# A scan with a gated linear unit on one core: a new written-out order of engines and transfers, with five gated buffers and separate gate loads

## The chip, the cores and the metric

The kernel runs on one core of one Trainium2 chip. Its time is device microseconds of one launch; the median of several runs is compared. A profile is one further execution, recorded by the hardware profiler, whose own time stands beside its span below.

## What is computed

Four sequences of 6336 tokens with 256 channels pass through a gated linear recurrence and then through a gated unit with a causal convolution of five taps.

```python
a_base  = sigmoid(a_param)
a_t     = exp(8 * sigmoid(r_gate) * log(clip(a_base, 1e-6, 1 - 1e-6)))
norm    = sqrt(max(1 - a_t * a_t, 1e-6))
x_gated = norm * sigmoid(i_gate) * x
h = a_t[:, t] * h + x_gated[:, t];  y[:, t] = h      # for each t, in float32
gate = sigmoid(causal_conv5(y, moe_conv_w))
out  = (gate * (y @ moe_w_val)) @ moe_w_out
```

x, r_gate, i_gate and the output are (4, 6336, 256) float32, 26 MB each. The weights are two 256 x 256 matrices, five rows of taps and one decay parameter per channel.

## The kernel before

The 25,344 tokens are cut into 27 chunks: one of 512, 23 of 1024, two of 512 and one of 256. A chunk passes through a pipeline over all engines. Steps up to the scan are by chunk c and channel half h; steps after it are by chunk and by part s of 512 tokens.

- `ldri`, `ldx` (L216 to L224): SyncE starts the loads of r and i, as a pair, into six gate slots (three chunks deep), and of x into two x slots.
- `tanh` (L290): ACT turns both gates into tanh(g/2), in bf16, in one instruction.
- `srT` (L295): TensorE transposes the r part to channel rows; `exp` (L304): ACT makes a from it, into a ring of five.
- `e` (L310): POOL squares a, into a ring of five; `sq` (L354): ACT makes the root of 1 - a*a, scaled by 1/4 inside. It is done for up to three chunks at a time, because it needs another function table than tanh and exp: a table load stands ahead of it and another behind it (L472).
- `s1` (L318): POOL adds 1 to the i part; `u` (L345): POOL multiplies it with x, into a ring of four gated buffers. For chunks 0 and 1 this is done another way: TensorE passes x through an identity in float32 (`xc`, L327) and VectorE does the sum and product from there (`ux`, L335).
- `nT` (L367), `xg` (L374), `xgT` (L382): TensorE transposes the root to token rows, VectorE multiplies the gated buffer with it in place, and TensorE transposes that back to channel rows.
- `scan` (L395): VectorE runs the recurrence along the tokens.
- `conv` (L407), `tg` (L417): TensorE does the five taps as matmuls with diagonal weights; ACT takes tanh into a ring of two.
- `val` (L425), `gv` (L430): TensorE multiplies with the first weight; VectorE forms the gated product into a second ring of two.
- `out` (L439), `osbD` (L454) or `osbA` (L450): TensorE multiplies with the second weight; VectorE or ACT copies the result to SBUF, into a ring of five.
- `store` (L459): ACT's queue starts the transfer to memory.

Ahead of the loop the decay constant is made from `a_param` by one exp, three small VectorE steps and one ln (L252 to L263). The weights are loaded once (`ldw`) and cast to bf16 by three ACT instructions (`wc`, L282 and L284).

The order is written out in the string `PLAN`, as names with chunk, part and PSUM bank. The program walks through it and emits one step after another under a manual schedule, so each engine, and each queue that starts transfers, works through its own steps in the order of the string. Waits between engines follow from the buffers: a load of r waits until `srT` has read the slot's former chunk, a load of i until `u` has, a load of x until `u` has read the x slot; a `u` waits until `xgT` has read the gated buffer's former chunk. Transfers of both queues (SyncE for loads, ACT for stores) share eight completion semaphores in turn, so one can also wait until an earlier transfer that has the same semaphore has landed.

The rings are set by numbers at the top.

```python
NRI = 3      # chunks of gate slots
NX = 2       # x
NA = 5       # a
NE = 5       # squares and roots
NU = 4       # gated buffers
NTG = 2      # tanh of the convolution
NGV = 2      # gated product
```

Of the kernel before, what the change touches and what calls it, by code (L numbers as in the profile page):

```python
# [8 lines left out]
P = 128  # L9
HP = 64  # L10
# [6 lines left out]
X_PE = [0, 1]  # L17
NRI = 3
NX = 2
NA = 5  # L20
NE = 5
NU = 4
NY = 3
NOSB = 5
NTG = 2
NGV = 2
# [7 lines left out]
ldri.0.-1 ldri.1.-1 ldx.0.-1 ldx.1.-1 ldri.2.-1 ldw.-1 tanh.0.-1 srT.0.0.7 srT.0.1.5 exp.0.1.-1 exp.0.0.-1 e.0.0.-1  # L34
tanh.1.-1 e.0.1.-1 xc.0.1.0 xc.0.0.6 ux.0.0.-1 xc.1.2.1 u.0.-1 sq.0.1.-1 ux.1.2.-1 srT.1.0.0 ldri.3.-1 xc.1.1.5
ldx.2.-1 nT.0.0.7 srT.1.1.4 exp.1.0.-1 xg.0.0.-1 ux.1.1.-1 exp.1.1.-1 xc.1.0.0 tanh.2.-1 xc.1.3.5 e.1.1.-1 ux.1.0.-1
e.1.0.-1 wc.-1 srT.2.0.3 s1.2.-1 srT.2.1.2 xgT.0.0.4 exp.2.0.-1 scan.0.0.-1 exp.2.1.-1 e.2.0.-1 u.1.-1 tanh.3.-1
ldx.3.-1 ldri.4.-1 e.2.1.-1 u.2.-1 srT.3.1.3 srT.3.0.6 xgT.0.1.1 sq.1.2.-1 s1.3.-1 ldx.4.-1 ldri.5.-1 nT.2.0.7
nT.2.1.0 u.3.-1 xg.2.0.-1 exp.3.1.-1 xg.2.1.-1 nT.1.1.7 scan.0.1.-1 nT.1.0.5 tanh.4.-1 xg.1.1.-1 conv.0.0.0 xg.1.0.-1
xgT.2.0.3 e.3.1.-1 ldx.5.-1 xgT.1.1.4 ldri.6.-1 xgT.1.0.2 scan.1.1.-1 tg.0.0.-1 exp.3.0.-1 s1.4.-1 srT.4.1.1  # L40
exp.4.1.-1 scan.1.0.-1 val.0.0.4 e.3.0.-1 tanh.5.-1 srT.4.0.6 gv.0.0.-1 conv.1.0.0 u.4.-1 scan.2.0.-1 xgT.2.1.7
tg.1.0.-1 srT.5.1.5 srT.5.0.4 exp.4.0.-1 scan.2.1.-1 val.1.0.0 exp.5.1.-1 e.4.1.-1 ldx.6.-1 ldri.7.-1 exp.5.0.-1
gv.1.0.-1 conv.2.0.6 tanh.6.-1 e.5.1.-1 out.0.0.4 conv.1.1.0 osbD.0.0.-1 e.4.0.-1 val.2.0.2 tg.1.1.-1 val.1.1.4
e.5.0.-1 store.0.0.-1 tg.2.0.-1 out.1.0.0 conv.2.1.6 osbD.1.0.-1 s1.5.-1 sq.3.3.-1 gv.1.1.-1 u.5.-1 gv.2.0.-1
out.2.0.0 out.1.1.4 osbD.2.0.-1 osbD.1.1.-1 s1.6.-1 nT.3.1.3 ldri.8.-1 nT.3.0.2 ldx.7.-1 val.2.1.0 tg.2.1.-1 xg.3.0.-1
xg.3.1.-1 store.1.0.-1 u.6.-1 tanh.7.-1 gv.2.1.-1 xgT.3.1.7 nT.4.0.6 scan.3.1.-1 srT.6.0.1 srT.6.1.4 xgT.3.0.2
nT.4.1.0 nT.5.1.5 exp.6.0.-1 xg.4.0.-1 s1.7.-1 ldri.9.-1 xg.4.1.-1 exp.6.1.-1 srT.7.0.1 xg.5.1.-1 ldx.8.-1 nT.5.0.6
scan.3.0.-1 exp.7.0.-1 out.2.1.4 e.6.1.-1 tanh.8.-1 xgT.4.1.3 srT.7.1.7 xg.5.0.-1 conv.3.0.0 e.7.0.-1 osbD.2.1.-1
scan.4.1.-1 conv.3.1.4 u.7.-1 store.1.1.-1 tg.3.0.-1 xgT.4.0.6 srT.8.0.2 tg.3.1.-1 scan.4.0.-1 srT.8.1.0 exp.7.1.-1
val.3.1.4 exp.8.1.-1 gv.3.1.-1 e.6.0.-1 conv.4.1.6 ldx.9.-1 exp.8.0.-1 ldri.10.-1 xgT.5.0.3 store.2.0.-1 tg.4.1.-1  # L50
out.3.1.4 e.7.1.-1 scan.5.0.-1 tanh.9.-1 xgT.5.1.7 val.3.0.0 e.8.0.-1 conv.4.0.2 gv.3.0.-1 osbD.3.1.-1 e.8.1.-1
tg.4.0.-1 scan.5.1.-1 val.4.1.4 s1.8.-1 val.4.0.0 sq.6.3.-1 out.3.0.2 gv.4.1.-1 u.8.-1 gv.4.0.-1 osbD.3.0.-1 out.4.0.0
out.4.1.2 osbD.4.0.-1 srT.9.1.6 osbD.4.1.-1 nT.8.1.5 s1.9.-1 ldri.11.-1 nT.6.1.4 xg.8.1.-1 exp.9.1.-1 conv.5.0.2
ldx.10.-1 xg.6.1.-1 store.3.0.-1 tanh.10.-1 e.9.1.-1 nT.6.0.4 nT.7.1.1 xg.6.0.-1 nT.7.0.0 xgT.6.1.5 xg.7.0.-1 u.9.-1
xgT.6.0.4 xg.7.1.-1 srT.9.0.6 scan.6.0.-1 nT.8.0.7 exp.9.0.-1 conv.5.1.0 tg.5.0.-1 scan.6.1.-1 tg.5.1.-1 xgT.7.1.2
s1.10.-1 ldri.12.-1 store.2.1.-1 tanh.11.-1 val.5.1.0 ldx.11.-1 xg.8.0.-1 srT.10.1.3 srT.10.0.6 gv.5.1.-1 e.9.0.-1
val.5.0.4 conv.6.1.0 gv.5.0.-1 exp.10.1.-1 u.10.-1 srT.11.1.7 scan.7.1.-1 store.3.1.-1 store.4.1.-1 conv.6.0.4
tg.6.1.-1 exp.10.0.-1 srT.11.0.1 xgT.7.0.0 tg.6.0.-1 val.6.0.2 scan.7.0.-1 exp.11.0.-1 e.10.0.-1 out.5.0.4 ldri.13.-1
store.4.0.-1 ldx.12.-1 exp.11.1.-1 osbD.5.0.-1 out.5.1.0 e.10.1.-1 tanh.12.-1 conv.7.0.6 osbD.5.1.-1 e.11.0.-1
val.6.1.4 gv.6.0.-1 gv.6.1.-1 out.6.0.2 tg.7.0.-1 e.11.1.-1 store.5.1.-1 osbD.6.0.-1 xgT.8.1.6 xgT.8.0.7 s1.11.-1  # L60
out.6.1.4 scan.8.1.-1 sq.9.3.-1 val.7.0.2 u.11.-1 gv.7.0.-1 osbD.6.1.-1 conv.7.1.2 scan.8.0.-1 srT.12.0.1 srT.12.1.6
nT.9.0.0 nT.9.1.4 s1.12.-1 ldri.14.-1 nT.11.0.5 xg.9.0.-1 exp.12.0.-1 nT.10.0.7 ldx.13.-1 xg.9.1.-1 store.6.1.-1
xg.11.0.-1 store.5.0.-1 tg.7.1.-1 xgT.9.1.0 e.12.0.-1 scan.9.1.-1 exp.12.1.-1 out.7.0.2 tanh.13.-1 val.7.1.4 u.12.-1
osbD.7.0.-1 conv.8.0.0 gv.7.1.-1 nT.10.1.2 xgT.9.0.3 xg.10.1.-1 tg.8.0.-1 srT.13.0.6 scan.9.0.-1 s1.13.-1 ldri.15.-1
store.7.0.-1 tanh.14.-1 val.8.0.0 ldx.14.-1 out.7.1.4 xg.10.0.-1 e.12.1.-1 conv.8.1.2 gv.8.0.-1 srT.13.1.7 osbD.7.1.-1
store.6.0.-1 tg.8.1.-1 u.13.-1 xgT.10.0.1 srT.14.0.0 scan.10.0.-1 exp.13.0.-1 srT.14.1.4 out.8.0.2 exp.14.0.-1
xgT.10.1.6 store.7.1.-1 osbD.8.0.-1 exp.13.1.-1 conv.9.0.0 e.14.0.-1 exp.14.1.-1 scan.10.1.-1 ldx.15.-1 val.8.1.2
ldri.16.-1 tg.9.0.-1 nT.11.1.7 val.9.0.4 e.13.0.-1 store.8.0.-1 tanh.15.-1 gv.8.1.-1 conv.9.1.0 gv.9.0.-1 e.14.1.-1
out.8.1.2 val.9.1.4 osbD.8.1.-1 tg.9.1.-1 e.13.1.-1 xg.11.1.-1 store.8.1.-1 gv.9.1.-1 xgT.11.0.3 out.9.0.0 s1.14.-1
sq.12.3.-1 scan.11.0.-1 out.9.1.6 xgT.11.1.5 u.14.-1 osbD.9.1.-1 osbD.9.0.-1 val.10.0.6 srT.15.1.4 scan.11.1.-1  # L70
conv.10.0.2 s1.15.-1 nT.12.1.1 ldri.17.-1 tg.10.0.-1 nT.12.0.0 xg.12.1.-1 ldx.16.-1 srT.15.0.5 exp.15.1.-1 xg.12.0.-1
conv.10.1.2 gv.10.0.-1 u.15.-1 exp.15.0.-1 xgT.12.0.0 val.10.1.6 scan.12.0.-1 tg.10.1.-1 nT.13.1.1 store.9.0.-1
tanh.16.-1 conv.11.0.4 gv.10.1.-1 nT.13.0.3 e.15.0.-1 ldri.18.-1 nT.14.0.0 xg.13.1.-1 out.10.1.6 ldx.17.-1 xg.14.0.-1
xg.13.0.-1 tg.11.0.-1 e.15.1.-1 srT.16.0.2 osbD.10.1.-1 out.10.0.0 tanh.17.-1 val.11.0.6 osbD.10.0.-1 s1.16.-1
xgT.12.1.3 gv.11.0.-1 srT.16.1.1 conv.11.1.4 u.16.-1 scan.12.1.-1 exp.16.1.-1 val.11.1.6 tg.11.1.-1 srT.17.1.0
exp.16.0.-1 gv.11.1.-1 xgT.13.0.5 srT.17.0.4 store.10.0.-1 exp.17.1.-1 conv.12.0.2 scan.13.0.-1 e.16.0.-1 ldri.19.-1
store.9.1.-1 exp.17.0.-1 nT.14.1.0 ldx.18.-1 xgT.13.1.7 tg.12.0.-1 xg.14.1.-1 e.17.1.-1 scan.13.1.-1 store.10.1.-1
tanh.18.-1 out.11.0.2 xgT.14.0.4 e.16.1.-1 conv.12.1.0 osbD.11.0.-1 val.12.1.6 scan.14.0.-1 e.17.0.-1 tg.12.1.-1
out.11.1.2 val.12.0.0 s1.17.-1 gv.12.1.-1 sq.15.3.-1 gv.12.0.-1 out.12.1.6 u.17.-1 osbD.11.1.-1 out.12.0.4
# [61 lines left out]
def kernel(  # L141
# [54 lines left out]
    with tc.manual_schedule():  # L196
# [16 lines left out]
        def slot(c, e):  # L213
            return 2 * (c % NRI) + e

        def op_ldri(k, bank):  # L216
            c = k[0]
            n = CHUNKS[c]
            for e, src in ((0, rf), (1, if_)):
# [287 lines left out]
```

## Time and profile before

| what | us |
|---|---|
| median of 3 runs | 310.08 (309.9 to 310.13) |
| the profiled execution's own time | 311.12 |
| its span in the profile | 309.0 |
| VectorE, scans (L395), 54 | 115.8 busy |
| ScalarE, gate tanh (L290), 27 | 90.2 busy |
| POOL, gated product u (L345), 25 | 96.0 busy |
| POOL, squares (L310), 54 | 93.6 busy |
| TensorE, conv matmuls (L407), 1224 | 65.3 busy |
| transfers, 104.74 MB | 339 GB/s over the span |

Busy time of an engine is the time in which at least one of its instructions ran; an instruction that overlaps its neighbour is counted once. A group of instructions shares a line, an engine and an operation. "Idle before" is the time an engine sat idle just ahead of an instruction, and the releaser is what the trace shows to have ended it. A store or a load is started by a queue (ACTq, SPq), which isn't counted as busy, and lands microseconds later.

### The profile page before, as it was taken

The page shows a single profiled execution, that of the slowest core. Times are in us where ns is not written, and L with a number is a line of the kernel's source. Part 1 is how long each engine was busy: PE and PEld are TensorE (multiplying, and loading weights), DVE is VectorE, ACT ScalarE, POOL GpSimd, SP SyncE. Part 2 cuts the span into 40 slices and gives each one's busy share as a digit, 9 for nine tenths or more (in the row PEclk, how much of TensorE's full clock was granted, in tenths as well). Part 3 has the DMA queues.
Part 4 walks back from the last instruction along what each step waited for, and adds up shares of the span by engine and source line. Part 5 has one row for each costly group of instructions (what it writes and reads, how often), then busy time and mean ns, then how long its engine had stood idle before and what let it go on. Part 6 is the DMA issues. An engine that isn't in the chain of part 4 may idle for free.

```text
span 309.0 us, 6335 instructions
## 1 busy us (share of the span) xinstructions
PE 248.1 (80%) x2627; PEld 167.7 (54%) x2627; DVE 252.3 (82%) x208; ACT 278.5 (90%) x185; POOL 235.2 (76%) x118
## 2 busy tenths in 40 slices
PE   0582577958888898799489998988899987999994
PEld 0232454447546564557257665675666655565763
DVE  1052079479898989999499999999999998989893
ACT  6799999999999999998699999999999979868632
POOL 3229998997998999899996799989959993038000
PEclk9995589999999999999979999999999999999999
DMA  7999999998997999999999997999897764182555
GB/s 288 427 360 422 382 417 364 365 352 318 389 377 263 413 414 422 421 421 421 428 423 365 363 390 280 376 426 424 336 369 309 285 249 137 69 337 109 200 212 237
DMA packets 19466, 104.74 MB, mean 339 GB/s; under 512 B 2151, under 2 KB 2670, under 8 KB 10606
## 3 DMA queue, kind: packets, MB, share of 16 engines
q1 hardware_dynamic: 12224, 78.39, 65.0%
q10 hardware_dynamic: 7214, 25.96, 21.0%
q8 instruction: 20, 0.33, 0.4%
q14 instruction: 8, 0.07, 0.1%
HBM read 78.39 MB, written 25.95 MB: 338 GB/s over the span
## 4 chain that ended last, share of the span: by engine, by line
PE 24%; DMA 21%; POOL 18%; ACT 17%; issue 11%; DVE 6%; ACTq 1%; SPq 1%; POOLq 0%; DVEq 0%
DMA gate<-in_i_gate_dram 13%; POOL uring L345 10%; PE pp L407 7%; PE pp L439 6%; DMA xr<-in_x_dram 6%; ACT gate L290 5%; POOL ering L310 5%; ACT tgr L417 4%; PE pp L425 4%; ACT aring L304 4%; POOL gate L318 3%; PE pp L367 3%; DMA out_dram<-osb 3%; DVE yring L395 3%; PE pp L327 2%
## 5 line engine op out<-in xcount | busy, mean ns | idle before, releaser
L310 POOL TENSOR_TENSOR ering<-aring 128x1024 f32<-128x1024 f32 (+2 forms) x54 | 93.6, 1754 | 36.7 <-ACT aring L304 35.1
L395 DVE TENSOR_TENSOR_SCAN yring<-aring,yring,pp 128x1024 bf16<-128x1024 f32 (+2 forms) x52 | 113.4, 2193 | 4.1 <-PE pp L382 4.1
L345 POOL TENSOR_TENSOR uring<-gate,xr 128x2048 bf16<-128x2048 bf16 (+2 forms) x25 | 96.0, 3845 | 4.3 <-PE pp L382 2.6
L290 ACT ACTIVATE gate<-gate 128x4096 bf16<-128x4096 f32 (+2 forms) x27 | 90.2, 3340 | 7.6 <-DMA xr<-in_x_dram 3.9
L407 PE MATMUL pp<-yring,diag 64*64 64x512 bf16 (+13 forms) x1224 | 65.3, 341 | 5.2 <-DVE yring L395 2.2
L430 DVE SCALAR_TENSOR_TENSOR gvr<-tgr,pp 128x1024 bf16<-128x1024 bf16 (+1 forms) x50 | 59.4, 1200 | 8.9 <-ACT tgr L417 6.7
L439 PE MATMUL pp<-wo,gvr 128*128 128x256 bf16 x396 | 52.7, 279 | 13.9 <-DVE gvr L430 7.9
L304 ACT ACTIVATE aring<-pp,khf 128x1024 f32<-128x1024 bf16 (+2 forms) x54 | 59.3, 1144 | 3.9 <-PE pp L295 2.2
L417 ACT ACTIVATE tgr<-pp 128x1024 bf16<-128x1024 f32 (+1 forms) x50 | 50.5, 1024 | 10.0 <-PE pp L407 8.6
L439 PEld LDWEIGHTS <-gvr 128*128 128x128 bf16 x396 | 42.5, 115 | 23.8 <-DVE gvr L430 11.1
L425 PE MATMUL pp<-yring,wv 128*128 128x512 bf16 (+1 forms) x200 | 50.5, 377 | 6.1 <-DVE osb L454 2.2
L454 DVE COPY osb<-pp 128x1024 f32<-128x1024 f32 x41 | 49.0, 1211 | 6.1 <-PE pp L439 5.9
L318 POOL TENSOR_SCALAR gate<-gate 128x2048 bf16<-128x2048 bf16 (+2 forms) x25 | 44.5, 1781 | 5.4 <-ACT gate L290 5.4
L407 PEld LDWEIGHTS <-diag 64*64 64x64 bf16 x1224 | 30.6, 107 | 30.6 <-issue 14.5
L354 ACT ACTIVATE ering<-ering,b 128x4096 bf16<-128x4096 f32 (+4 forms) x16 | 46.4, 2932 | 0.1
L374 DVE TENSOR_TENSOR uring<-uring,pp 128x1024 bf16<-128x1024 bf16 (+1 forms) x50 | 32.0, 672 | 12.7 <-PE pp L367 12.5
L295 PE MATMUL pp<-ident_b,gate 128*128 128x128 bf16 x396 | 31.4, 229 | 13.2 <-ACT gate L290 11.1
L295 PEld LDWEIGHTS <-gate 128*128 128x128 bf16 x396 | 26.6, 103 | 21.9 <-ACT gate L290 14.0
L367 PE MATMUL pp<-ident_f,ering 128*128 128x128 f32 x198 | 32.3, 303 | 5.4 <-ACT ering L354 3.9
L382 PE MATMUL pp<-ident_f,uring 128*128 128x128 f32 x198 | 31.5, 282 | 6.1 <-ACT tgr L417 2.8
L367 PEld LDWEIGHTS pp<-ident_f,ering 128*128 128x128 f32 x198 | 27.8, 208 | 11.6 <-ACT ering L354 4.8
L425 PEld LDWEIGHTS <-wv 128*128 128x128 bf16 x200 | 18.8, 98 | 23.9 <-issue 11.1
(33 smaller groups left out, 86.9 us busy)
## 6 DMA issues: line engine op xcount, KB each, us to landing
out_dram<-osb ACTq DMA_DIRECT2D x49, 512.0 KB, 7.9
gate<-in_r_gate_dram SPq DMA_DIRECT2D x23, 1024.0 KB, 11.7
gate<-in_i_gate_dram SPq DMA_DIRECT2D x23, 1024.0 KB, 9.6
xr<-in_x_dram SPq DMA_DIRECT2D x23, 1024.0 KB, 10.0
gate<-in_r_gate_dram SPq DMA_DIRECT2D x3, 512.0 KB, 7.7
gate<-in_i_gate_dram SPq DMA_DIRECT2D x3, 512.0 KB, 10.7
xr<-in_x_dram SPq DMA_DIRECT2D x3, 512.0 KB, 3.4
yring<-in_moe_w_val_dram SPq DMA_DIRECT2D x1, 256.0 KB
```

The source lines that it names most:

```text
L290: nc.scalar.activation(out=tgate[:, s0:s0 + 2, 0:w], in_=gate[:, s0:s0 + 2, 0:w], func=ACT.Tanh, scale=0.5)
L295: nc.tensor.transpose(out=ppb[:, bank * 2 * BANK + j * P:bank * 2 * BANK + (j + 1) * P], in_=tgate[:, slot(c, 0), j * D + h * P:j * D + (h ...
L304: nc.scalar.activation(out=dst, in_=src, func=ACT.Exp, scale=khf[:, h:h + 1], bias=khf[:, h:h + 1])
L310: nc.gpsimd.tensor_tensor(out=ering[:, c % NE, h * n:(h + 1) * n], in0=a, in1=a, op=ALU.mult)
L345: nc.gpsimd.tensor_tensor(out=u, in0=t, in1=xt, op=ALU.mult)
L367: nc.tensor.transpose(out=pp[:, d0:d0 + P], in_=src[:, w, :], identity=ident_f[:])
L395: nc.vector.tensor_tensor_scan(out=yring[:, h, y0:y0 + n], data0=aring[:, c % NA, h, 0:n], data1=src, initial=prev, op0=ALU.mult, op1=ALU.add)
L407: nc.tensor.matmul(out=pp[col * HP:(col + 1) * HP, b0 + d0:b0 + d1], lhsT=diag[r * HP:(r + 1) * HP, h, kk, :], rhs=yring[r * HP:(r + 1) * ...
L417: nc.scalar.activation(out=tgr[:, nth[k] % NTG, :, 0:n], in_=two(live["conv", k], n), func=ACT.Tanh, scale=0.5)
L425: nc.tensor.matmul(out=pp[:, (bank + m) * BANK:(bank + m) * BANK + n], lhsT=wv[:, hk, m, :], rhs=yring[:, hk, y0:y0 + n], start=(hk == 0), ...
L430: nc.vector.scalar_tensor_tensor(out=gvr[:, nth[k] % NGV, :, 0:n], in0=tgr[:, nth[k] % NTG, :, 0:n], scalar=1.0, in1=two(live["val", k], n ...
L439: nc.tensor.matmul(out=pp[:, bank * BANK + j * D:bank * BANK + (j + 1) * D], lhsT=gvr[:, nth[k] % NGV, m, 0:n].rearrange("c (p q) -> c q p ...
```

## The change

The order string is another one throughout, and with it come some changes of code. In words:

- `ldri` is split into `ldr` and `ldi`, which stand in the string by themselves. Loads start with r of chunk 0, i of 1, i of 0, r of 1. Later, loads of r stand one or two chunks ahead of loads of i (r of 7, 8 and 9, then i of 7 and x of 6, then i of 8).
- A common function `dma` starts all transfers, and adds an edge from each transfer to the one before it in the string, across both queues. The edge is of a kind that makes no semaphore wait; it holds the order in which the transfers are taken.
- POOL leaves the set of engines of the manual schedule; its instructions are wrapped in `keep`, which holds them in the order of the program.
- `X_PE` is empty: chunks 0 and 1 get `s1` and `u` on POOL like the others, and `xc` and `ux` go.
- `NU` is 5 for 4. `gvr` goes: `gv` writes in place of `tg`'s result, whose ring is 3 for 2.
- `tanh` of chunk 0 is two instructions (`tanh` for r, `tanhi` for i).
- The weight casts `wc` go from ACT to POOL.
- The decay constant is made by exp, ln(1 + v) and two VectorE steps after it, with the limits of the clip moved behind the logarithm. Three small VectorE steps ahead of it go. Some constants are put into the last output buffer until it is first used.
- Of the 50 output copies ACT makes 14 for 9 (parts 17.0, 18.0, 22.0, 22.1 and 24.0 and 23.1 are added, 20.1 is taken away), VectorE 36 for 41.
- Stores stand in groups at places: 0.0, 1.0, 1.1 and 2.0 follow each other on ACT's queue after `tanh` of chunk 7 and ahead of one `exp` and `tanh` of chunk 8; 8.1, then one `exp`, then 9.0, 9.1 and 10.0 stand ahead of `tg` of 11.0 and `tanh` of chunk 16.
- On POOL, `u` of chunks 4, 7, 10 and 13 stands behind the four squares of the two chunks after it in the root's batch, which it preceded, in whole or in part, before.

The root's batches are the same (chunk 0; 1 and 2; then threes; 21 and 22; 23 and 24; 25 and 26), and the number of table loads too (24). The diff, cut to its core:

```diff
-X_PE = [0, 1]
+X_PE = []
-NU = 4
+NU = 5
-NTG = 2
-NGV = 2
+NTG = 3
...
-    with tc.manual_schedule():
+    with tc.manual_schedule(engines={mybir.EngineType.SP, mybir.EngineType.Activation, mybir.EngineType.DVE,
+                                     mybir.EngineType.PE}):
...
-        def op_ldri(k, bank):
+        keep = tc.keep_in_program_order
+        turn = []
+
+        def dma(queue, dst, src):
+            i = queue.dma_start(dst, src)
+            if turn:
+                tc.add_manual_dep(i.ins, turn[-1].ins.name,
+                                  mybir.DependencyInfo(mybir.DependencyClass.NoSync, mybir.DependencyReason.DATA),
+                                  reason="turn of the transfers")
+            turn.append(i)
+
+        def op_ldr(k, bank):
             c = k[0]
             n = CHUNKS[c]
-            for e, src in ((0, rf), (1, if_)):
-                nc.sync.dma_start(gate[:, slot(c, e), 0:n * H].rearrange("p (j d) -> p j d", d=D), toks(src, c, 0, n))
+            dma(nc.sync, gate[:, slot(c, 0), 0:n * H].rearrange("p (j d) -> p j d", d=D), toks(rf, c, 0, n))
+
+        def op_ldi(k, bank):
+            c = k[0]
+            n = CHUNKS[c]
+            dma(nc.sync, gate[:, slot(c, 1), 0:n * H].rearrange("p (j d) -> p j d", d=D), toks(if_, c, 0, n))
...
-        nc.vector.tensor_scalar(out=ksig[:], in0=kex[:], scalar1=1.0, scalar2=None, op0=ALU.add)
-        nc.vector.reciprocal(out=ksig[:], in_=ksig[:])
-        nc.vector.tensor_scalar(out=ksig[:], in0=ksig[:], scalar1=1e-6, scalar2=1.0 - 1e-6,
-                                op0=ALU.max, op1=ALU.min)
-        nc.scalar.activation(out=kln[:], in_=ksig[:], func=ACT.Ln)
+        nc.scalar.activation(out=kln[:], in_=kex[:], func=ACT.Ln, bias=1.0)
...
         def op_wc(k, bank):
             for hk in range(H):
-                nc.scalar.copy(out=wv[:, hk, :, :].rearrange("p m (i c) -> p i m c", i=2),
-                               in_=wvf[:, hk, :].rearrange("p (i m c) -> p i m c", i=2, m=2))
-            nc.scalar.activation(out=wo2[:], in_=wof, func=ACT.Copy, scale=0.5)
+                keep(nc.gpsimd.tensor_scalar(out=wv[:, hk, :, :].rearrange("p m (i c) -> p i m c", i=2),
+                                             in0=wvf[:, hk, :].rearrange("p (i m c) -> p i m c", i=2, m=2),
+                                             scalar1=1.0, scalar2=1.0, op0=ALU.mult, op1=ALU.mult))
+            keep(nc.gpsimd.tensor_scalar(out=wo2[:], in0=wof, scalar1=0.5, scalar2=1.0, op0=ALU.mult, op1=ALU.mult))
...
-            s0 = slot(c, 0)
-            nc.scalar.activation(out=tgate[:, s0:s0 + 2, 0:w], in_=gate[:, s0:s0 + 2, 0:w], func=ACT.Tanh, scale=0.5)
+            s0, s1 = slot(c, 0), slot(c, 0) + (1 if c == 0 else 2)
+            nc.scalar.activation(out=tgate[:, s0:s1, 0:w], in_=gate[:, s0:s1, 0:w], func=ACT.Tanh, scale=0.5)
+
+        def op_tanhi(k, bank):
+            c = k[0]
+            w = CHUNKS[c] * H
+            nc.scalar.activation(out=tgate[:, slot(c, 1), 0:w], in_=gate[:, slot(c, 1), 0:w], func=ACT.Tanh, scale=0.5)
...
-            nc.gpsimd.tensor_tensor(out=u, in0=t, in1=xt, op=ALU.mult)
+            keep(nc.gpsimd.tensor_tensor(out=u, in0=t, in1=xt, op=ALU.mult))
...
-            nc.vector.scalar_tensor_tensor(out=gvr[:, nth[k] % NGV, :, 0:n], in0=tgr[:, nth[k] % NTG, :, 0:n], scalar=1.0,
+            nc.vector.scalar_tensor_tensor(out=tgr[:, nth[k] % NTG, :, 0:n], in0=tgr[:, nth[k] % NTG, :, 0:n], scalar=1.0,
                                            in1=two(live["val", k], n), op0=ALU.add, op1=ALU.mult)
...
-            nc.scalar.dma_start(toks(of, c, o, n),
-                                osb[:, nth[k] % NOSB, 0:n // P * D].rearrange("p (q d) -> p q d", d=D))
+            dma(nc.scalar, toks(of, c, o, n), osb[:, nth[k] % NOSB, 0:n // P * D].rearrange("p (q d) -> p q d", d=D))
```

## The prediction, made before the changed kernel was run

> **What bounds the kernel now.** I read the page first: busy shares, then the span in forty slices.
>
> ```profile
> PE 248.1 (80%) x2627; PEld 167.7 (54%) x2627; DVE 252.3 (82%) x208; ACT 278.5 (90%) x185; POOL 235.2 (76%) x118
> ...
> PE   0582577958888898799489998988899987999994
> DVE  1052079479898989999499999999999998989893
> ACT  6799999999999999998699999999999979868632
> POOL 3229998997998999899996799989959993038000
> ```
>
> ACT has the most work, and its idle 30.5 us (309.0 - 278.5) lies at the two ends and in one dip near slice 19. No engine is at rest in the middle. So I asked for the busy time by stage.
>
> ```profile
> 0.00:60.00 60.00, 35.83 (x272) 22.25 (x273) 23.31 (x27) 53.81 (x37) 41.73 (x27) 0.86 0.96 379
> 60.00:100.00 40.00, 30.92 (x333) 22.27 (x333) 35.96 (x30) 39.90 (x23) 37.05 (x18) 1.00 0.92 341
> 100.00:160.00 60.00, 48.62 (x523) 32.92 (x522) 53.97 (x41) 55.55 (x33) 58.13 (x27) 0.97 1.02 420
> 160.00:250.00 90.00, 81.95 (x921) 57.01 (x919) 88.95 (x70) 89.66 (x57) 80.41 (x37) 1.00 0.92 356
> 250.00:309.00 59.00, 50.72 (x584) 33.24 (x584) 50.14 (x43) 39.53 (x39) 17.85 (x13) 0.99 0.49 190
> ```
>
> The columns are the stretch, its length, then the busy us of PE, weight load, DVE, ACT and POOL, the granted clock, the share of the transfers and GB/s. Four regimes follow. To 60 us the pipeline fills and the DMA is nearly full (0.96). From 100 to 160 the DMA is full (420 GB/s) and ACT loses 4.45 us. From 160 to 250 ACT (89.66 of 90) and DVE (88.95) are full together. From 250 on ACT has 19.5 us idle, while DVE (50.14) and PE (50.72 of 59) carry the backlog; finer stretches show PE at 10.00 of 10.00 from 280 to 290 and from 290 to 300. The timeline of ACT shows the loss near 146:
>
> ```profile
> 144.80 1.07 ACT L417 ACTIVATE tgr<-pp 128x1024 bf16<-128x1024 f32 x1
> 149.31 0.34 ACTq L459 DMA_DIRECT2D out_dram<-osb  x1
> 149.78 3.62 ACT L290 ACTIVATE gate<-gate 128x4096 bf16<-128x4096 f32 x1 [3.90 <-DMA xr<-in_x_dram]
> ```
>
> The gate tanh of chunk 15 doesn't read x. A store stands ahead of it on ACT's queue, and its issue came at 149.31, just before the tanh starts. In the compiled order that store waits for the transfer some eight earlier to land. The tanh itself needs i of chunk 15, issued only at 136.0, when POOL's gate product of chunk 12 had freed the slot. Late release, a full DMA, and waits on an engine's queue: that is one loss of 3.90 us.
>
> **What the Trainium skill says.** "DMA: Bandwidth & Descriptors", section Anatomy of one DMA: the wait of a transfer is done by the sequencer that issues it, before dispatch; the trace agrees, with SyncE's queue waiting 88.7 us for POOL at L220 and the tanh above behind a store. Same page, Where 436 GB/s comes from: a ceiling of 435 GB/s; the best 20 us stretch here, 140 to 160, moved 424. "Advanced Engine Details and Errata", section Engine Queue Depths: eight instructions for ScalarE; the trace fits, since a store was issued at 62.97 while a sqrt from 61.21 was still running, so a short wait at a store need not idle ACT.
>
> **The change part by part.** The sum is made against the profiled execution: span 309.0 in a time of 311.12, 1.04 above the median 310.08. I carry differences in us over to the median unchanged.
>
> *Head, -1.9.* The weight casts leave ACT: 0.69 + 0.63 = 1.3 us (L282, L284), on ACT's own path from the first tanh on. The six x matmul groups (L327, 12 instructions, 8.8 us of PE) and six DVE products (L335, 4.2 us) go. They lie where DVE sat idle 10.69 us, so DVE gains nothing; PE's release takes with it the 0.60 us that ACT waited for a transpose behind them. The other head waits of ACT (0.54, 1.13, 0.48, 1.03) I leave: r, i of chunk 1 still need the same 3.0 MB ahead, chunk 2 the same 6.5 MB. The split tanh of chunk 0 and the three DVE steps gone from the decay constant (0.17 each) end before that load lands: nothing. Bounds: 0 and -(1.3 + 3.8) = -5.1.
>
> *POOL, 0.* It receives s1 and u of chunks 0 and 1 (1.05 + 2.16 + 1.90 + 4.12 = 9.2 us) and the weight casts, 1024 elements a partition. L318 has 1.90 us for 2048 bf16 elements, so 0.95; at the two-input fp32 price of the "GPSIMD Engine Reference", section Performance versus the Vector engine (4497 ns for 2048), 2.25. I take 1.0. POOL is idle 3.76 us before 10.3 and 8.85 us before 21.2, which covers the 9.2; without that cover u of chunk 2, and the loads behind it, come 9.2 later. The casts stand after those gaps, ahead of u of chunk 3, the step that frees i and x slots: 0 to +2.25 there, taken as 0: u of chunk 3 ended at 40.9, a load of i takes 9.6, and the tanh of chunk 6 started only at 54.4.
>
> *Loads, -2.0.* r and i no longer go as a pair. r of chunks 8 and 9 is put ahead of i of chunk 7, and so on: r needs only PE's transposes done, i needs POOL's u. The fifth gated buffer lets u run one chunk further ahead of the transposes back (POOL waited 2.6 us for these). The number of loads, 84 on SyncE, and the bytes stay. To 160 us the DMA was busy 0.96 x 60 + 0.92 x 40 + 1.02 x 60 = 155.6 us, so at most 4.4 us of earlier arrival is there; the head has taken 1.9 of it. Of ACT's stalls of 3.90 and 0.45 I take 2.0 back; bounds 0 and -4.35. Against it: in POOL's new order u of every third chunk (4, 7, 10, 13) stands behind four squares, 4 x 1.87 = 7.5 us later, and i of the third chunk after waits for it.
>
> *Copies, +1.0.* ACT makes 14 output copies for 9. Two of them (17.0, 18.0) lie in the stage where ACT is full: 2 x 1.01 = 2.0. DVE, just as full, loses 2 x 1.21. Bounds 0 and +2.0; I take the middle.
>
> *DVE and the backlog, -3.0.* Net five copies of 1.211 leave DVE, 6.05 us. What is late next is PE: it was idle 90 - 81.95 = 8.05 us from 160 to 250 and 2.12 + 1.35 + 0.38 = 3.85 from 250 to 300, mostly waiting for DVE and ACT. DVE's relief can turn at most 6.05 of these 11.9 into work; I take half. Bounds 0 and -6.05.
>
> *Stores and turns, 0.* The edges between transfers add no waits of their own (the compiled order shows none across the queues), but they fix which earlier transfer each one waits for. Stores now stand up to four in a row on ACT: 0.0, 1.0, 1.1 and 2.0 after the tanh of chunk 7, with an exp and the tanh of chunk 8 behind them and all POOL work on chunk 8 behind these; 9.0, 9.1 and 10.0 likewise ahead of the tanh of chunk 16. Each is worth 0 (transfer eight earlier landed) to 3.9 us (the stall above). Less than nothing it can't be here, since that gain is counted under the loads. I take 0, since the copies for most of them end well before.
>
> *One ring for tg and gv, 0.* tg now waits for the output matmuls three steps back instead of a DVE product two back: between -1.3 (ACT's present wait for L430) and +1.0 (one group of L439).
>
> Table loads stay at 24 in both orders. Sum: -1.9 - 2.0 + 1.0 - 3.0 = -5.9: 305.2 for the profiled execution, **304.2** for the median.
>
> **The rivals.**
> - *PE keeps the end where it is*: the DVE relief meets a PE that is full at 10.00 of 10.00 from 280 on, and gives nothing: 310.1 - 1.9 - 2.0 + 1.0 = 307.2. For it: PE has no copy taken away. Against: 8 us of its idle lie before 250.
> - *Everything comes through*: both stalls and all of DVE's relief, copies free: 310.1 - 1.9 - 4.35 - 6.05 = 297.8. Against: ACT alone has 278.5 - 1.3 + 5.0 = 282 us of work, and this leaves it only some 15 us idle.
> - *Slower: stores hold ACT.* One mechanism: a store on ACT's queue waits for a transfer eight back, the tanh behind it waits too, and POOL and the next loads with it. Price 3.9 us a time. It decides from 5.9 / 3.9 = 1.5, so from two new stalls: 304.2 + 7.8 = 312.0. For it: four stores in a row. Against: the queue holds several instructions, and only one of 50 stores cost ACT such a stall before.
> - *No effect*: DMA-bound to 160, PE-bound after, only the places of waits change: 310.1.
>
> **How the numbers follow.** Forecast 304.2 with 0.52, PE at the end 0.20, everything 0.13, stores 0.11, no effect 0.04. A change of 0.2% (0.6 us) is about what a measurement can tell from none. Faster is the first three, 0.85; same 0.04; slower 0.11. The range leaves out the stores and the no-effect case (0.15) and reaches from just below the best case to just under no change: 297.5 to 309.4.
>
> **What would show it.** Right: ACT idle from 100 to 160 falls from 4.45 to about 2.5; the third square root batch starts near 59, not 61.2 (1.9 earlier); DVE busy about 241; PE idle from 160 on falls by some 3. Wrong: POOL idle before a u at a wait for x, ACT gaps just behind L221 stores, or a tail after the last gate tanh longer than now.

## The result and the profile after

| | us, median | runs |
|---|---|---|
| before | 310.11 | 309.9 to 311.11 |
| after | 319.31 | 317.74 to 319.62 |

The ratio is 1.028 (95% interval 1.0239 to 1.0321): slower by 9.2 us, where 304.2 was predicted. The profiled execution of after took 319.1 us, with a span of 317.3: 8.3 us longer than the span before. First, the same lines of the page as before:

```profile
PE 244.4 (77%) x2585; PEld 170.9 (54%) x2615; DVE 243.4 (77%) x195; ACT 283.2 (89%) x188; POOL 245.6 (77%) x125
...
PE   1153385785898888899849967999779999998994
DVE  0030179379987999899668988699998999989972
ACT  6798999999999999997977978999898899889754
POOL 3898997989998799899867989994999854743000
```

The work moved as the diff says. VectorE has 8.9 us less, POOL 10.4 more, ScalarE 4.7 more. But the 9s of ACT's row break up from slice 20 on, where the row before was solid. The stages show the same in microseconds; the columns are again stretch, length, busy us of PE, weight load, DVE, ACT and POOL, clock, share of the transfers and GB/s.

```profile
0.00:60.00 60.00, 28.45 (x258) 21.20 (x261) 18.14 (x19) 53.21 (x35) 50.06 (x33) 1.00 0.90 368
60.00:100.00 40.00, 30.93 (x317) 22.15 (x316) 34.20 (x28) 38.43 (x22) 38.40 (x18) 0.96 0.93 360
100.00:160.00 60.00, 52.26 (x588) 36.19 (x588) 55.06 (x44) 57.63 (x35) 54.78 (x25) 1.00 0.94 371
160.00:250.00 90.00, 73.18 (x759) 51.53 (x772) 79.53 (x63) 80.59 (x49) 77.32 (x36) 0.94 0.94 369
250.00:317.30 67.30, 59.62 (x687) 39.85 (x684) 56.42 (x46) 53.34 (x50) 25.06 (x16) 0.98 0.50 190
```

From 100 to 160 us ScalarE's idle time fell from 4.45 to 2.37 us, as predicted. From 160 to 250 it rose from 0.34 to 9.41 us; VectorE's busy time fell by 9.4 there and TensorE's by 8.8. This stage loses what the whole change costs.

A second way to count needs no borders of stages. ScalarE runs the square roots in eleven batches, the same in both kernels, and from the start of the last batch to its last instruction it takes 22.4 us before and 22.1 after. So the end follows from that start, which is ScalarE's busy time ahead of it plus its idle time ahead of it. Before: 266.2 + 17.4 = 283.6. After: 268.1 + 24.2 = 292.3. The change adds 1.9 us of work and 6.8 us of idle time ahead of the last roots. The largest piece lies between the sixth batch of roots and the seventh: 6.9 us for 0.1. The other pieces nearly cancel. The stretch from the sixth batch to the seventh, first before, then after:

```profile
155.60:186.40 30.80, 28.50 (x315) 19.43 (x313) 30.20 (x23) 30.73 (x20) 26.43 (x12) 0.97 1.00 384
156.10:202.10 46.00, 34.52 (x369) 23.76 (x371) 36.47 (x28) 39.06 (x24) 38.55 (x16) 0.93 0.97 387
```

(The new order also puts 8.3 us more of ScalarE's work into this stretch; later stretches have less.)

What was waited for? The waits of SyncE's queue, which starts all loads; first before, then after. The columns are who waits, for whom, us in all, times and the longest.

```profile
SPq L220 <- POOL uring L345: 88.7, 12, 13.7
SPq L224 <- POOL uring L345: 73.0, 9, 18.4
SPq L502 <- DMA out_dram<-osb: 27.6, 5, 21.4
```

```profile
SPq L221 <- POOL uring L364: 117.1, 20, 13.9
SPq L221 <- DMA out_dram<-osb: 59.5, 11, 12.4
SPq L520 <- DMA out_dram<-osb: 41.5, 5, 35.4
```

L502 and L520 are the end of the program and don't count. L221 is the new common `dma`, so the second line is new: 11 times a *load* stood on SyncE's queue until a *store* had landed, 59.5 us in all. No load did so before. A store and a load share no buffer; they share a completion semaphore. Four of the eleven, from the compiled order of the transfers and the trace (times in us; "eight back" is the transfer that had the same semaphore before):

```
load  ready to issue  issued  what stands eight back  that started  landed
x14   142.1           148.1   store 5.1               138.8         148.1
i17   161.7           166.6   store 8.0               151.9         166.6
x17   177.5           184.4   store 10.0              168.8         184.4
r23   212.4           224.8   store 12.1              217.8         224.8
```

Each of these loads is issued in the moment the store lands. The stores took 9.3, 14.7, 15.6 and 7.0 us. The chain of waits that ended last carries one of these four, 10.0 (the second line), and ahead of it store 7.1:

```profile
144.29 18.59 DMA out_dram<-osb
...
168.79 15.64 DMA out_dram<-osb
```

Store 7.1 does its harm elsewhere. Part 10.0 uses its output buffer (ring of five), so VectorE's copy of 10.0 waits for it to land. The timeline from 158 us on (start, duration, engine, line; in brackets the idle time ahead and what ended it):

```profile
163.00 1.22 DVE L473 COPY osb<-pp 128x1024 f32<-128x1024 f32 x1 [2.49 <-DMA out_dram<-osb]
...
164.28 0.66 PE L401 MATMUL pp<-ident_f,uring 128*128 128x128 f32 x4 [4.53 <-DVE osb L473]
...
167.58 1.20 ACT L323 ACTIVATE aring<-pp,khf 128x1024 f32<-128x1024 bf16 x1 [2.59 <-PE pp L314]
```

VectorE loses 2.49 us, TensorE 4.53 (the bank that the copy frees), ScalarE 2.59. Without the edges (run 1 below) this is where the two traces part; up to 160 us the stages of the table above agree within 0.4 us on every engine. In run 1 the same copy waits 0.70 us.

### The profile page after: what moved, and what is told of

The parts are those of the page before. It is cut to its first block, busy times and chain, and to the rows that moved or that the text cites. A ratio compares the mean times of both kernels' runs of the same rounds, so it can differ in the third digit from the quotient of the medians.

```text
span 317.3 us, 6301 instructions
## 1 busy us (share of the span) xinstructions
PE 244.4 (77%) x2585; PEld 170.9 (54%) x2615; DVE 243.4 (77%) x195; ACT 283.2 (89%) x188; POOL 245.6 (77%) x125
## 4 chain that ended last, share of the span: by engine, by line
PE 25%; DMA 19%; ACT 16%; POOL 14%; DVE 12%; issue 10%; ACTq 1%; SPq 0%; DVEq 0%; POOLq 0%
DMA out_dram<-osb 11%; PE pp L426 7%; POOL uring L364 6%; DMA gate<-in_i_gate_dram 6%; DVE yring L414 5%; PE pp L386 5%; POOL ering L329 5%; ACT ering L373 5%; PE pp L458 5%; ACT gate L304 4%; PE pp L444 4%; POOL gate L337 3%; DVE osb L473 3%; ACT tgr L436 3%; DMA gate<-in_r_gate_dram 3%
## 5 line engine op out<-in xcount | busy, mean ns | idle before, releaser
L329 POOL TENSOR_TENSOR ering<-aring 128x1024 f32<-128x1024 f32 (+2 forms) x54 | 93.9, 1752 | 30.7 <-ACT aring L323 25.9
L364 POOL TENSOR_TENSOR uring<-gate,xr 128x2048 bf16<-128x2048 bf16 (+2 forms) x27 | 102.2, 3789 | 8.1 <-DMA xr<-in_x_dram 7.5
L426 PE MATMUL pp<-yring,diag 64*64 64x512 bf16 (+14 forms) x1224 | 65.6, 344 | 10.6 <-DVE yring L414 6.6
L449 DVE SCALAR_TENSOR_TENSOR tgr<-tgr,pp 128x1024 bf16<-128x1024 bf16 (+1 forms) x50 | 59.3, 1201 | 17.1 <-ACT tgr L436 8.1
L314 PE MATMUL pp<-ident_b,gate 128*128 128x128 bf16 x396 | 35.0, 241 | 24.7 <-ACT gate L304 19.1
L458 PE MATMUL pp<-wo,tgr 128*128 128x256 bf16 x396 | 50.6, 274 | 4.1 <-DVE tgr L449 3.2
L337 POOL TENSOR_SCALAR gate<-gate 128x2048 bf16<-128x2048 bf16 (+2 forms) x27 | 47.4, 1756 | 2.0 <-ACT gate L304 1.9
L473 DVE COPY osb<-pp 128x1024 f32<-128x1024 f32 x36 | 43.4, 1212 | 7.2 <-DMA out_dram<-osb 4.8
L458 PEld LDWEIGHTS <-tgr 128*128 128x128 bf16 x396 | 41.7, 114 | 13.3 <-DVE tgr L449 7.0
L314 PEld LDWEIGHTS <-gate 128*128 128x128 bf16 x396 | 29.0, 109 | 32.3 <-ACT gate L304 24.7
L386 PE MATMUL pp<-ident_f,ering 128*128 128x128 f32 x198 | 35.7, 325 | 11.0 <-ACT ering L373 7.0
## 6 DMA issues: line engine op xcount, KB each, us to landing
xr<-in_x_dram SPq DMA_DIRECT2D x23, 1024.0 KB, 10.9
```

The lines of the kernel that those rows point to most:

```text
L314: nc.tensor.transpose(out=ppb[:, bank * 2 * BANK + j * P:bank * 2 * BANK + (j + 1) * P], in_=tgate[:, slot(c, 0), j * D + h * P:j * D + (h ...
L329: keep(nc.gpsimd.tensor_tensor(out=ering[:, c % NE, h * n:(h + 1) * n], in0=a, in1=a, op=ALU.mult))
L364: keep(nc.gpsimd.tensor_tensor(out=u, in0=t, in1=xt, op=ALU.mult))
L386: nc.tensor.transpose(out=pp[:, d0:d0 + P], in_=src[:, w, :], identity=ident_f[:])
L426: nc.tensor.matmul(out=pp[col * HP:(col + 1) * HP, b0 + d0:b0 + d1], lhsT=diag[r * HP:(r + 1) * HP, h, kk, :], rhs=yring[r * HP:(r + 1) * ...
L449: nc.vector.scalar_tensor_tensor(out=tgr[:, nth[k] % NTG, :, 0:n], in0=tgr[:, nth[k] % NTG, :, 0:n], scalar=1.0, in1=two(live["val", k], n ...
```

## The experiments

All times are medians beside runs of the kernel before on the same chip (309.9 to 310.6). "Old order" is the order string of before, "new code" everything else of the change. Line numbers differ between runs where the string fills more lines: `dma` is L221 or L248.

The expectations name theories by letter. A: the edges make loads wait for stores. B: the order string itself costs the time. C: the new code does. D and E: the output copies, on ScalarE or on VectorE. F: the ceiling of the transfers. G: the groups of stores hold output buffers.

| run | order | edges | other | us | ratio (95%) |
|---|---|---|---|---|---|
| 1 | new | no | as after | 315.0 | 1.0159 (1.0132 to 1.0186) |
| 2 | old | no | new code | 319.6 | 1.0306 (1.0280 to 1.0333) |
| 3 | old | yes | new code | 316.5 | 1.0189 (1.0144 to 1.0234) |
| 4 | new | no | copies as before | 319.3 | 1.0297 (1.0248 to 1.0347) |
| 5 | new | no | four u earlier | 316.2 | 1.0198 (1.0139 to 1.0257) |
| 6 | old | no | new code, u of 1 early | 311.2 | 1.0026 (1.0005 to 1.0048) |
| 7 | old | yes | as 6 | 307.2 | 0.9880 (0.9814 to 0.9945) |
| 8 | new | yes | loads ahead in the turn | 316.5 | 1.0183 (1.0145 to 1.0222) |
| 9 | new | yes | quarter stores | 309.7 | 0.9967 (0.9946 to 0.9989) |
| 10 | old | no | before, quarter stores | 304.2 | 0.9802 (0.9780 to 0.9823) |
| 11 | old | yes | as 7, rings mended | 306.3 | 0.9870 (0.9845 to 0.9895) |
| 12 | new | no | 39 stores early | 324.6 | 1.0444 (1.0403 to 1.0485) |
| 13 | new | yes | 39 stores early | 323.9 | 1.0448 (1.0403 to 1.0492) |
| 14 | new | no | quarter stores | 308.6 | 0.9943 (0.9922 to 0.9964) |
| 15 | old | yes | as 11, new copies | 307.4 | 0.9917 (0.9886 to 0.9949) |
| 16 | new | yes | 5 stores early | 316.1 | 1.0176 (1.0132 to 1.0219) |
| 17 | new | no | 5 stores early | 314.7 | 1.0151 (1.0116 to 1.0186) |
| 18 | old | yes | before, edges alone | 307.2 | 0.9908 (0.9877 to 0.9938) |

In runs 2, 3, 6 and 7 the ring of three is one too short for the old order: parts 3.0, 5.0 and 22.0 take the gated product of another part. No work is left out there. Runs 9, 10 and 14 leave out three quarters of the output. All others leave nothing out.

### Runs 1 to 3: the edges or the order

```diff
-            if turn:
-                tc.add_manual_dep(i.ins, turn[-1].ins.name, ...)
```

> The kernel after, without the edges between transfers; the order on every engine and on both queues, the buffers and the code stay as they are, and only the way the eight completion semaphores are handed round between loads and stores changes. Theory A (the edges make loads wait for stores eight places back): the loads of x14, i17, x17 and r23 no longer wait 5 to 12 us for a store to land, ScalarE's idle time between 160 and 250 us falls from 9.4 us to under 3, and the time is 304 to 311 us. Theory B (the order string itself costs it: four u of POOL behind their squares, loads of r far ahead, stores in groups): the time stays at 317 to 320 us, with the same gaps. Theory C (the new code: u of chunks 0 and 1 and the casts on POOL, five gated buffers): stays at 317 to 320 us too.

> The code of the kernel after with the order string of the kernel before (both gates loaded as a pair, u at its old places, stores at theirs; the steps xc and ux are replaced by s1 and u on POOL), without the edges. Theory A: about the time of the kernel before, 306 to 312 us, as nothing makes loads wait for late stores. Theory B: 306 to 312 us too, as the order is the old one. Theory C: 314 to 320 us, as the code is the new one.

> As the run before it, but with the edges between transfers. Theory A in its strong form (any order pinned by edges makes loads wait for stores): 313 to 320 us. In its weak form (it needs this string's places of stores and loads): 306 to 312 us. Theory B: 306 to 312 us. Theory C: 314 to 320 us, as without edges.

Run 1: 315.0. The edges cost 4.3 of the 9.2 us, and theory A's signs are there. On SyncE's queue no load waits for a store; the only such line left is the program's end. ScalarE's idle time between the sixth and the seventh roots is 2.8 us (41.60 - 38.84) for 6.9:

```profile
SPq L516 <- DMA out_dram<-osb: 40.9, 5, 34.8
```

```profile
156.10:197.70 41.60, 33.41 (x379) 22.97 (x377) 37.20 (x29) 38.84 (x24) 37.54 (x16) 1.00 1.01 417
```

But 5 us stay, so A isn't all.

Runs 2 and 3 seemed to speak for C, the new code. Their traces say otherwise. ScalarE's timeline of run 2 has one large stall in the head, and POOL's shows why:

```profile
37.08 3.71 ACT L359 ACTIVATE ering<-ering,b 128x4096 bf16<-128x4096 f32 x1 [5.06 <-POOL ering L315]
```

```profile
20.36 3.74 POOL L315 TENSOR_TENSOR ering<-aring 128x1024 f32<-128x1024 f32 x2 [6.34 <-ACT aring L309]
...
29.12 1.90 POOL L323 TENSOR_SCALAR gate<-gate 128x2048 bf16<-128x2048 bf16 x1
31.10 4.10 POOL L350 TENSOR_TENSOR uring<-gate,xr 128x2048 bf16<-128x2048 bf16 x1
35.14 1.91 POOL L315 TENSOR_TENSOR ering<-aring 128x1024 f32<-128x1024 f32 x1
```

I had put s1 and u of chunk 1 (6.0 us at 29.1) ahead of the second square of chunk 2, which the second batch of roots waits for, while POOL stood idle for 6.34 us earlier. That was a fault of these two kernels, not of the new code; the next runs mend it. The edges, harmful in the new order, gained 3 us here.

### Runs 4 to 7: parts of the order, and the old order mended

```diff
-osbA.17.0 osbA.18.0 osbA.22.0 osbA.22.1 osbA.23.1 osbA.24.0 osbD.20.1    (run 4)
+osbD.17.0 osbD.18.0 osbD.22.0 osbD.22.1 osbD.23.1 osbD.24.0 osbA.20.1
-e.3.0 e.4.1 e.5.1 e.5.0 e.4.0 u.4     (run 5; 7, 10 and 13 likewise)
+e.3.0 u.4 e.4.1 e.5.1 e.5.0 e.4.0
-e.0.1 s1.0 u.0 ... s1.2 e.2.0 s1.1 u.1 e.2.1     (runs 6 and 7, against 2 and 3)
+e.0.1 s1.0 u.0 s1.1 u.1 ... s1.2 e.2.0 e.2.1
```

In runs 6 and 7 the weight casts also go behind s1 of chunk 3.

> The kernel after without the edges (315.0 us), and with the output copies divided as in the kernel before: 17.0, 18.0, 22.0, 22.1, 23.1 and 24.0 go back to VectorE, 20.1 goes to ScalarE. Theory D (what is left of the loss, some 5 us, is ScalarE's work: five more copies of 1.0 us on an engine that has no idle time to take them): 310 to 312 us, with ScalarE's busy time down by 5. Theory B (the places of u, the loads and the stores): 313 to 316 us, as ScalarE waits at the same places. Rival E (VectorE takes the place of ScalarE): 315 to 317 us.

> The kernel after without the edges (315.0 us), and with u of chunks 4, 7, 10 and 13 moved to where the old order has them, ahead of the squares of the two later chunks of the batch. Theory B in the form that a late u of 8 to 11 us delays the loads of x and i behind it: the wait of u of 15 for its x (about 3.8 us) and the ScalarE gaps of 160 to 190 us go, and the time is 311 to 313 us. Theory D: 314 to 316 us. Rival: the roots of the batch come later by up to 4 us each, as the squares are what they wait for, and the time is 316 to 320 us.

> The old order with the new code and without the edges, with s1 and u of chunk 1 on POOL ahead of the squares of chunk 1, where the old order made it on VectorE; in the two runs before it u of chunk 1 stood behind a product of VectorE that used it, and the head of the kernel lost 7 us to that. Theory B or D (the loss lies in the new order): 306 to 311 us. Theory C (POOL's 10 us of added work in the head): the third batch of roots starts at 64 us or later, for 61.2, and the time is 312 to 316 us.

> As the run before it with the edges between transfers. In the two old-order runs before the edges made it 3 us faster (316.5 for 319.6). Theory A in its weak form (the edges do harm only where the string places stores eight transfers ahead of loads that have to come soon): the same as without edges or up to 3 us less, 304 to 311 us. Theory A in its strong form: 3 us or more above the run without edges.

The reason that run 6's expectation gives for the head is wrong; it is the one shown above.

Run 4 refutes D: with the five copies back on VectorE the kernel is 4.3 us slower than run 1, not faster. ScalarE's work ahead of the last roots falls by 0.5 us only, and its idle time there rises from 19.9 to 22.8. So the copies are well placed on ScalarE in the new order. Run 5, 1.2 us above run 1 with overlapping intervals, gives no sign that the late u has a part in the loss; its profile is of its slowest execution, 318.5, and isn't compared.

Run 6 is 0.9 us above before (ratio 1.0026, at most 1.0048), so the new code in itself costs about 1 us in the old order, and C as the cause of the 5 us falls too. Run 7 adds the edges and gains 4 us. The edges are good for one string and bad for another: A holds in its weak form. (Run 11 below, with a ring that is long enough, lies within 1 us of run 7, so the short ring isn't what makes run 7 fast.)

### Runs 8 to 11: other turns, smaller stores

```diff
-dma(nc.scalar, toks(of, c, o, n), osb[...])            (runs 9, 10, 14)
+dma(nc.scalar, toks(of, c, o, n)[:, 0:1, :], osb[...][:, 0:1, :])
-NU = 5                                                  (run 11, against 7)
-NTG = 3
+NU = 4
+NTG = 4
```

Run 8 changes only places in the string: each load is moved up to just behind the step that frees its slot, in the same order.

> The kernel after with its edges and with every engine's and both queues' order as it is; only the place of each load in the string is moved up to where its slot becomes free, so loads stand ahead of stores in the turn, and other transfers stand eight places ahead of them (x14 behind i16's group, i17 behind s6.0 for s8.0, x17 behind no store for s10.0). Theory A (what the edges cost, 4.3 us, is loads that wait for stores that have not landed): 313 to 316 us, as without edges. If the edges cost time in another way (stores on ScalarE's queue that now wait for loads): 318 to 322 us.

> The kernel after, of whose stores only a quarter is written (one row of 1 KB for each partition in place of four; the rest of the output is left out), so that 19% of the bytes go and the number, the order and the waits of transfers stay. Theory F (between 130 and 220 us the transfers run at their ceiling of about 420 GB/s, and the 2.4 MB that the new order moves too little between 100 and 130 us cannot be made up): the time falls to 305 to 309 us, near that of the kernel before with the same cut. Theory A gives a gain of 4 to 5 us too, as stores land sooner. Theory B without the transfers (the order of POOL, VectorE and ScalarE alone): 316 to 320 us.

> The kernel before with the same cut of its stores (three quarters of the output are left out). Theory F: it has been close to the ceiling of the transfers as well, but with few holes, so it gains 1 to 4 us, to 306 to 309 us, and the difference between the two orders shrinks from 9 us to under 3. Theory B without the transfers: 308 to 310 us, and the difference to the run before stays at 7 us or more.

> The old order with the new code and the edges, with the one ring of tanh and gated product at four in place of three (the old order needs that many at once) and the gated buffers at four again to make room; u of chunks 0 and 1 and the casts on POOL. Nothing is left out. If the gain of the run with three (307.2 for 310.3 us) came from the edges and the new code: 305 to 308.5 us, faster than both kernels. If five gated buffers were part of it: 309 to 311 us.

Run 8 keeps the edges but pins another turn: 3 us of the 4.3 come back, and SyncE's waits for stores are gone. What costs isn't the edges as such, but the turn that they pin.

Runs 9 and 10 say how much is due to full-sized stores: 9.6 us in after, 6.0 in before. The ranges were passed on the slow side in run 9 and on the fast side in run 10, so theory F is half right: both kernels lose to transfers, and the 5.5 us that stay between them are something else. (Runs 9 and 14 scatter, 306 to 312 us; the medians are of 20 runs.) Run 11 leaves nothing out and beats both kernels: 306.3, ratio 0.987.

### Runs 12 to 15: stores at once, and the copies in the old order

```diff
-tg.2.0 tg.1.0 ... store.5.0 ... store.5.1 store.6.0 ... store.6.1 store.7.0
+(each store ahead of the first ScalarE step that began 0.3 us or more after its copy)
```

> The kernel after without the edges (315.0 us), and with each store moved to the first place on ScalarE's queue that comes after its copy is done, in place of the groups (39 of the 50 stores move ahead by 1 to 11 ScalarE steps; everything else keeps its order). Theory G (the groups hold output buffers: VectorE's copies of parts 9.1 and 10.0 wait for stores five parts back to land, and VectorE's wait goes on to TensorE and ScalarE): the wait of VectorE's copies for stores, 2.9 us, goes, ScalarE's idle time from 156 us to the next roots falls from 2.7 us to about 1, and the time is 311 to 313 us. If stores sent early take the transfers' time from the loads instead: 315 to 318 us.

> The kernel after with its edges (319.3 us), and each store moved ahead in the same way. Theory A with G (what the edges cost is loads waiting for stores that were started late and so land late; a store started 5 to 15 us sooner has landed by then): 312 to 315 us, and the loads' wait for stores on SyncE's queue, 59.5 us in all, falls to under 20. If the edges cost time whatever the place of the stores: 318 to 321 us.

> The kernel after without the edges and with a quarter of each store written (three quarters of the output are left out). With the edges this was 309.7 us, the kernel before 304.2 us. Theory A with nothing else in the transfers (the edges' 4 us are the whole of it): 305.5 to 307 us. If the edges cost nothing once stores are small, since small stores land in 6 to 9 us less: 308.5 to 310.5 us, and then the 5 us between the two orders with small stores is engine work and waits among engines alone.

> The old order with the new code, the edges and the rings of run 11 (306.3 us), and with the new order's choice of output copies: 17.0, 18.0, 22.0, 22.1, 23.1 and 24.0 on ScalarE, 20.1 on VectorE. In the new order these copies on ScalarE were worth 4.3 us. If that holds in general: 303 to 305.5 us. If ScalarE is the bound of the old order up to its last roots, each copy ahead of them costs 1.0 us: 307 to 311 us.

Runs 12 and 13 lie above every expectation, by 6.6 and 2.9 us. In run 12 VectorE's waits for stores did go (2.9 us to none), and the idle time from 156 us to the next roots fell to 0.9. But ScalarE's waits have new lines:

```profile
ACT L513 <- DVE uring L416: 4.9, 2, 3.0
ACT L513 <- DVE osb L496: 4.4, 4, 1.7
```

L513 is a table load. It needs nothing from VectorE; ahead of it on the queue stands a store whose copy wasn't done. The places came from run 1's times, the steps shifted, and stores held ScalarE for 9.3 us. So 324.6 says nothing of G. It shows what a store that comes too early costs.

Run 14: without edges and with quarter stores 308.6, against 309.7 with edges. The 4.3 us shrink to 1.0, and the intervals of the two ratios overlap. That fits a cost that comes from stores that take long to land; but with small stores the loads have 19% fewer bytes beside them too, so this run doesn't tell the two apart.

Run 15: in the old order the same copies on ScalarE cost some 1 us (306.3 to 307.4, intervals overlapping), where they gain 4.3 in the new one (run 4 to run 1).

### Runs 16 to 18: five stores, and the edges alone

```diff
-tg... store.5.0 ... store.5.1 store.6.0 ... store.6.1 store.7.0     (runs 16 and 17)
+store.5.0 (7 ScalarE steps sooner) store.5.1 (8) store.6.0 (8) store.6.1 (7; 6 in run 17) store.7.0 (1)
-                nc.sync.dma_start(...)                              (run 18, on before)
+                dma(nc.sync, ...)
```

> The kernel after with its edges (319.3 us), and only the stores of parts 5.0 to 7.0 moved ahead on ScalarE's queue, by 7, 8, 8, 7 and 1 steps, to the first place at least 3 us after their copy is done, so that none should hold ScalarE as the 39 moved stores did in the two runs before. Theory G (that group holds output buffers): VectorE's waits for stores at 152 to 163 us (0.5, 1.8 and 2.5 us) go, x14 and i16 no longer stand behind s5.1 and s6.1, and the time is 314.5 to 317 us. If the group costs nothing that counts: 318 to 321 us.

> The same five stores moved ahead, without the edges (315.0 us with the group). Theory G: VectorE's 2.9 us of waits for stores go, ScalarE's idle time between the roots at 156 us and the next falls from 2.7 us to about 1, and the time is 312.5 to 314 us. If the group costs nothing that counts, or the loads lose to the stores what the copies gain: 314.5 to 317 us.

> The kernel before with one part of the change alone: the edges between transfers (and what they need, POOL outside of the manual schedule with its order kept). The order string, the buffers and the code are those of before; nothing is left out. If the edges are what made the old order faster with the new code (311.2 to 307.2 us): 305 to 308 us, with ScalarE's idle time between 122 us and the roots at 156 us down from 4.0 to about 1.2 us. If that gain needed the new code: 309 to 312 us.

Run 16: with the edges, these five stores are worth 3.2 us (319.3 to 316.1). Its profile is of its fastest execution, 313.3, so its microseconds aren't compared with medians. Run 17: without the edges they are worth nothing (315.0 to 314.7). With this group moved the edges cost 1.4 us (316.1 with them, 314.7 without) for 4.3, so the edges' cost and this group are one and the same loss for the most part. VectorE's waits for stores are gone in both. SyncE's queue in run 16:

```profile
SPq L248 <- DMA out_dram<-osb: 36.9, 9, 12.4
```

The waits of r15, x14 and i16 (18.7 us together in after) are gone, and i17's fell from 8.8 to 3.5. 36.9 us of waits are left, those of x17 (6.8) and r23 (12.4) among them, and with all of them run 16 is only 1.4 us above run 17. In after, i of chunk 23, which the same tanh needs, was issued 9 us later than r23, so that wait can't count. The sum of a queue's waits is no price. Which single load's wait costs the time isn't shown; r15, x14, i16 and i17 are those that changed most.

For the five stores that give nothing without edges, the trace of run 17 offers a reason. Stores 5.1, 6.0 and 6.1 start at 123.7 to 128.3 us, and i14, started at 129.0, lands only at 140.5. The tanh of chunk 14, which needs it, starts then:

```profile
137.40 1.05 ACT L459 ACTIVATE tgr<-pp 128x1024 bf16<-128x1024 f32 x1
140.49 0.34 ACTq L248 DMA_DIRECT2D out_dram<-osb  x1
140.95 3.62 ACT L327 ACTIVATE gate<-gate 128x4096 bf16<-128x4096 f32 x1 [2.50 <-POOL ering L352]
```

The releaser named, a square on POOL, has nothing to do with this tanh; the load that landed at 140.5 has. Run 1's tanh of chunk 14 started at 139.6, though all ahead of it was 1.3 us later. What VectorE gains from the stores, a load seems to lose to them, as the expectation's second case has it; that is read from one profile. G's own sign failed: VectorE's 2.9 us of waits went, but ScalarE's idle time between the sixth and the seventh roots stayed at 2.6 us for 2.8.

Run 18: the edges alone make the kernel before 2.7 us faster. The 3.90 us stall of the prediction's third excerpt is now:

```profile
145.77 0.34 ACTq L221 DMA_DIRECT2D out_dram<-osb  x1
146.21 3.62 ACT L302 ACTIVATE gate<-gate 128x4096 bf16<-128x4096 f32 x1 [1.12 <-DMA gate<-in_i_gate_dram]
```

Before, store 8.0 had x14 eight back, which landed at 149.2; with the edges it has i15, landed at 145.7, which the tanh needs anyway. Of 3.90 us 2.8 are gone, and the kernel gains 2.7. A load behind a store and a store behind a load are the same mechanism from its two sides.

## Why the prediction was wrong

Measured and forecast differ by 15.1 us (319.3 and 304.2). The edges, priced at 0, are 4.3 of them; this step is shown. The other 10.8 are the rest of the sum, forecast at -5.9 and measured at about +5 without the edges; of these, the cause of the 5 us stays open.

- **Stores and turns, 0: the step that is shown to have failed, by 4.3 us.** It said that the edges "add no waits of their own" but "fix which earlier transfer each one waits for", and then priced the stores alone, as a hold on ScalarE's queue. The other half, loads behind stores on SyncE's queue, wasn't looked at. In the compiled order of after 20 loads have a store eight ahead. Before there are 22, but the view shows no wait of a load for a store; in after 11 waits add up to 59.5 us. Which store stands ahead of which load could be read from the compiled order, but not how late it lands. Run 1 (4.3 us), run 8 (2.9 with another turn) and runs 16 and 17 (3.2 and 0.3) show it.
- **The rival "slower: stores hold ACT"** had the sign, not the mechanism. ScalarE's large gaps in after stand behind TensorE and loads of i, none behind a waiting store. The price was real all the same: the kernel before pays it once, and run 18 got it back.
- **Loads, -2.0: right where it was read, then lost.** ScalarE's 4.45 us from 100 to 160 became 2.37, by 2.1. The roots at 156 us still began 0.5 us later than before: ScalarE had lost 1.5 us more between the roots at 61 and 91 us and 0.6 more ahead of them, and had 0.6 us more work. The next stage then lost 9 us. A sign of being wrong came true here: POOL sat idle 4.4 us before u of chunk 15, waiting for x (3.8 without the edges), where it never waited for x between 60 and 280 us before.
- **Head, -1.9: too large.** The third roots began at 60.9 for 61.2, so 0.3. ScalarE's work ahead of them fell by 0.9 us only, and its idle time grew from 6.2 to 6.8.
- **One ring, 0: held.** ScalarE's 1.3 us of waiting for L430 went, and no wait for the output matmuls came.
- **POOL, 0: held.** u of chunk 2 starts at 30.7 in both; runs 2 and 3 show what the cover was worth. The casts took 0.77 + 0.61 us.
- **Copies, +1.0, and VectorE, -3.0.** As a pair -2.0; in the new order -4.3 (run 4 against 1), in the old about +1 (run 15 against 11). "DVE busy about 241" was 243.4; the backlog stayed, 22.4 us to 22.1 from the last roots on. TensorE's idle time from 160 us on, forecast to fall by 3, rose from 16.3 to 24.5. So the relief of VectorE was no relief of the end.
- **The sum itself.** Without edges the new order is still 5 us slower than before, and with small stores 4.5 to 5.5 (runs 14 and 9 against 10), where the other terms summed to -5.9. By run 1's profile (3.5 us above that of before) it is 1.7 us more work and 2.5 us more idle time of ScalarE ahead of the last roots, in gaps of under 2 us, mostly at `tg` waiting for TensorE's conv matmuls (11.2 us in 15 waits; before 8.6 in 7). The late u (run 5), the copies (run 4) and the new code (run 6: about 1 us) don't explain it. From 100 to 130 us the new order leaves the transfers a hole, with or without edges: a busy share of 0.86 for 1.01 before. That isn't all either, since 4.5 us stay with small stores. TensorE's new order was not tried alone, so the cause stays open. A term for "the string is another one throughout" was missing, and with it the range's upper end.

## What to carry to other kernels

These runs show it for one kernel. Where transfers of several queues share completion semaphores in turn, write down for each transfer what stands a full turn ahead of it on either queue, when that starts and how long it takes to land; a load that is needed at once should not have a late store there, nor a store on a busy engine's queue a late load. An edit that pins the order of transfers can have either sign with one and the same line of code (-2.7 and +4.3 us here), so try it alone. In these runs a store was best neither as early as can be nor in late groups: early it holds its queue until the copy is done, or takes the transfers from a load that is needed next; late it holds its buffer and its semaphore.

## What was not expected of the hardware

- Stores of 512 KB (8.0, 10.0 and 7.1) took 14.7 to 18.6 us to land where loads of 1 MB were started around them; the median of all stores was 7.2 us, and of the 1 MB loads 7.5 to 10.9. The transfers' busy share was 0.89 to 1.02 in the stretches of 10 us from 140 to 190 us.
- The order in which a program hands out semaphores, with no instruction moved on any queue, is worth some 3 to 4 us of 310 (4.3 in run 1, 2.9 in run 8, 2.7 in run 18).
- Leaving out 19% of the bytes gained 6.0 us in the kernel before, whose ScalarE showed 3.9 us of stalls at transfers in its middle; its idle time ahead of the last roots fell from 17.4 to 10.9 us.
